# Attention output with the values and the state stationary: one head per column group, and the result transposed back

## The chip, the cores and the metric

The kernel runs on one NeuronCore of one Trainium2 chip. The metric is the time of one execution on the device, in microseconds (us). The kernel before was timed in three runs: 531.51, 533.49 and 534.09 us, median 533.49 us.

## The reference

Four batches, eight heads, 768 positions, 48 values per head. A gated linear attention comes first: a state of 48 x 48 per head decays by `alpha` and takes in the outer product of key and value at each position, and the output is the query times the state. Then the eight heads are laid side by side (384 columns), mixed by a Fourier transform over positions and columns, normalised, and sent through a feed-forward net with 384, 1536 and 384 columns.

```python
for t in range(S):
    state = alpha[:, :, t, :, None] * state + np.einsum('bhd,bhe->bhde', k[:, :, t], v[:, :, t])
    y[:, :, t] = np.einsum('bhd,bhde->bhe', q[:, :, t], state)
...
u = x + np.real(np.fft.fft(np.fft.fft(x, axis=1), axis=2))
un = (u - mean(u)) / np.sqrt(var(u) + 1e-06)
out = u + np.maximum(un @ w_ch1, 0.0) @ w_ch2
```

## The kernel before, in words

The attention is done for a pair of heads at a time, 16 pairs in all, four to a batch. Channels lie on the partitions: head 0 on partitions 0 to 47, head 1 on 64 to 111, so that a tile of a pair spans 112 partitions (`CW`); positions lie along the rows, in six blocks of 128. The stages of a pair (`attn_stages`) are:

- `s1` to `s3`: running products of `alpha` by two scans on VectorE (DVE), then keys divided by them (kept in the tile `al`) and queries multiplied by them (kept in a `w` tile, called `e["A"]`).
- `s4`: TensorE (PE) transposes the scaled keys, ScalarE (ACT) copies them to `kt`.
- `s5`: scores, keys times queries within a block of 128 positions. The two heads lie on different partitions, 48 or 64 rows each, and their matmuls stand next to each other in the program. ACT copies each head's scores from PSUM (into a tile `X`: `x` in the first batch, `w` later), GpSimd (POOL) masks them.
- `s6`: the state after each block. PE multiplies the transposed keys (stationary, 112 columns) by the values of both heads (moving, 96 columns): five matmuls. The products of one head's keys with the other's values are not wanted; two small ACT instructions make the decay factors `mh` with a zero for the wrong head, and a DVE product with them writes the tile `tt` of 112 partitions and 2 x 48 columns a block, with zeros for the wrong head. Four DVE instructions add up the blocks.
- `s7`: the output. For each block and head PE multiplies the scores (stationary, 128 columns) by the values (moving, 64 columns), and adds the queries (stationary, 112 rows and 128 columns) times the state `tt` (moving, 96 columns, both heads at once). The result has positions on the partitions, and ACT copies it to the tile `y`.

`combine` then prepares the transform on DVE; `mix_stages` does it on PE, `norm_stages` normalises, `ffn_stages` runs the feed-forward net. Its matmuls are the `f<-x,wt` and `f<-wt,h` of the profile: 128 x 128 stationary, 384 columns moving, 864 of each.

The order is made by a planner (`Plan`). Every operation is recorded with a duration from a formula (`duration`), a key and its dependencies; `emit` then places them one by one, on each engine the one with the smallest key among those that can start, and the engines run them in that order. The matmuls of a batch's feed-forward net have larger keys than the next batch's attention: they fill the time in which the attention waits. Up to `WARM` = 120 us of planned time the planner also puts small matmuls of zeros (128 rows, 32 columns stationary and moving, line 1130) where PE would be idle. Since one helper issues every operation, nearly all rows of the profile say line 471, and operations are told apart by their tiles. In a row, what stands after `<-` are the moving and then the stationary operand, and `128*112 128x96` is rows x columns of the stationary operand and rows x columns of the moving one. A matmul in float32 is two records.

A matmul uses a part of the PE array that follows from its operands: rows 48 or 64 (`s5`) give a shape of 64 rows, an output of 48 or 64 partitions a shape of 64 columns, one of 32 a shape of 32 columns; all else is the full array of 128 x 128.

Of the kernel before, what the change touches and what calls it, by code (L numbers as in the profile page):

```python
# [16 lines left out]
AF = mybir.ActivationFunctionType  # L17
ALU = mybir.AluOpType
AX = mybir.AxisListType

B, H, S, D = 4, 8, 768, 48
DM = H * D
DFF = 4 * DM
P = 128
NT = S // P
# [5 lines left out]
CW = 112  # L31
GRP = 64
# [141 lines left out]
class Plan:  # L174
# [119 lines left out]
    def duration(self, op, named, engine):  # L294
        n = op.free
        if "dma" in op.name:
            return 1.05 if engine == "POOL" else 0.05
        if engine == "PE":
            m = self.region(named["1"])[4]
            if op.name == "transpose":  # L300
                return max(m, self.region(named["2"])[4]) / 1200 + 0.002
            if str(named["1"].real(self.base(named["1"])).dtype).endswith("float32"):
                slow = 1.65 if self.stride(named["2"]) > 16 else 1.0
                p0, p1 = self.region(named["1"])[0:2]
                return max(m, slow * n) / (1100 if p1 - p0 <= GRP else 600) + 0.004
            return n / 2240 + 0.003
        if engine == "ACT":
            pointer = 0.094 if any(isinstance(named.get(k), View) for k in ("bias", "scale")) else 0.0
            slow = 1.8 if self.stride(named["out"]) > 16 and n > 64 else 1.0
            return (0.11 if self.psum(named.get("1")) else 0.14) + slow * n / 1200 + pointer + (0.25 if "accum_out" in named else 0.0)  # L310
        if op.name == "memset":
            return n / (960 if engine == "DVE" else 1100) + 0.01
        if engine == "DVE":
            if op.name == "bn_stats":
                return 0.47
            if op.name == "reciprocal":
                return 0.07 + n / 160
            if op.name == "tensor_tensor_scan":
                return 0.1 + n / 480
            if isinstance(named.get("scalar1"), View):  # L320
                return 0.09 + n / 1200
            whole = "bitcast" in [s[0] for s in named.get("out", View(None)).steps]
            pointer = 0.06 if isinstance(named.get("scalar"), View) else 0.0
            return 0.09 + pointer + n / (1920 if whole and op.name == "tensor_scalar" else 960)
        return 0.126 + n / 1094 if op.name == "affine_select" else 0.15 + n / 477
# [163 lines left out]
def gla_mix_ffn(ctx: ExitStack, tc: tile.TileContext, alpha, kq, v, w1, w2, consts, rowtab, out):  # L489
    nc = tc.nc  # L490
    plan = Plan({"PE": nc.tensor, "ACT": nc.scalar, "DVE": nc.vector, "POOL": nc.gpsimd, "SP": nc.sync})
    V, A, G, T, SY = (Engine(plan, e) for e in ("DVE", "ACT", "POOL", "PE", "SP"))
    FL = {k: Engine(plan, *[{"V": "DVE", "G": "POOL", "A": "ACT"}[c] for c in x]) for k, x in FX.items()}
# [31 lines left out]
    def psa():  # L525
        if state["start"]:
            state["i"] += 1
            return plan.tile(start_tags[state["i"] % 8])
        return plan.tile("a")
# [8 lines left out]
    def fixed(shape, name, dtype=F32):  # L538
        return plan.fixed(cp.tile(shape, dtype, name=name))
# [3 lines left out]
    ident = cst[:, ID_O : ID_O + P]  # L543
    wts = [None] * (NW // 2)
    loaded = {}
    tts = [fixed([P, NT - 1, 2, D], f"tt{i}") for i in range(2)]
    mhs = [fixed([P, NT - 1, 2], f"mh{i}") for i in range(2)]
    mts = [fixed([P, NT], f"mt{i}") for i in range(3)]
    d1 = fixed([P, S], "d1")
    back = fixed([P, S], "back")  # L550
# [3 lines left out]
    ceps = fixed([P, 1], "ceps")  # L554
    zero = fixed([P, 32], "zero")
    ones = fixed([P, 1], "ones")
    hm = fixed([P, 2], "hm")
    rows = fixed([P, 3], "rows", I32)
    bs = fixed([P, 1], "bs")
    fl = fixed([1, 1], "fl", I32)  # L560
# [42 lines left out]

    def setup():
        V.memset(zero, 0.0)
        for hd in range(2):
            V.memset(hm[GRP * hd : GRP * (hd + 1), hd : hd + 1], 1.0)
            V.memset(hm[GRP * (1 - hd) : GRP * (2 - hd), hd : hd + 1], 0.0)
        V.memset(d1, 0.0)
        V.memset(back, 0.0)  # L610
        V.memset(back[:, C - 1 :: 2 * C], 1.0)
        V.memset(cm63, -63.0)
        V.memset(ceps, 1e-6)
        for x in mts:
            V.memset(x, 0.0)
        V.memset(ones, 1.0)
        V.memset(bad, 0.0)
# [42 lines left out]
    def attn_stages(b, hp, i, mixed):  # L660
        tt, mt = tts[i], mts[hp % 3]
        pair = b * NP2 + hp
        e = {}
# [80 lines left out]
        def s6():  # L744
            pu = psa()
            for a in range(NT - 1):
                T.matmul(pu[0:CW, a * 2 * D : (a + 1) * 2 * D], e["kt"][:, a], loaded["vn", pair][:, 2 * a * D : 2 * (a + 1) * D], start=True, stop=True)
            mh = mhs[i]
            for hd in range(2):
                A.activation(mh[0:CW, :, hd], mt[0:CW, 0 : NT - 1], AF.Copy, scale=hm[0:CW, hd : hd + 1])  # L750
            V.tensor_tensor(
                out=tt[0:CW], in0=pu[0:CW, 0 : (NT - 1) * 2 * D].rearrange("p (a h e) -> p a h e", h=2, e=D),
                in1=mh[0:CW, :, :, None].broadcast_to([CW, NT - 1, 2, D]), op=ALU.mult,
            )
            for a in range(1, NT - 1):
                V.scalar_tensor_tensor(
                    out=tt[0:CW, a], in0=tt[0:CW, a - 1], scalar=mt[0:CW, a : a + 1], in1=tt[0:CW, a], op0=ALU.mult, op1=ALU.add,
                )

        def s7():  # L760
            X = e["X"]
            ytiles = mixed()[0]
            for h2 in range(2):
                py = psa()
                for c in range(3):
                    cc = 3 * h2 + c
                    cs = slice(cc * P, (cc + 1) * P)
                    o = c * 2 * GRP
                    for hd in range(2):
                        T.matmul(  # L770
                            py[:, o + hd * GRP : o + (hd + 1) * GRP], X[h2][:, hd, c], loaded["vn", pair][:, (2 * cc + hd) * D : (2 * cc + hd) * D + GRP],
                            start=hd == 0, stop=cc == 0 and hd == 1,
                        )
                    if cc:
                        yo = py[:, o : o + 2 * GRP].rearrange("p (h e) -> p h e", h=2)[:, :, 0:D]
                        T.matmul(yo, e["A"][0:CW, cs], tt[0:CW, cc - 1], start=False, stop=True)
                yo = py[:, 0 : 6 * GRP].rearrange("p (a h e) -> p a h e", a=3, h=2)[:, :, :, 0:D]
                FL["ev"].copy(ytiles[h2][:, :, hp * 2 * D : (hp + 1) * 2 * D].rearrange("p a (h e) -> p a h e", h=2), yo)

        return [s1, s2, s3, s4, s5, s6, s7, lambda: combine(*mixed(), hp * 2 * D, 2 * D, FL["comb"])]  # L780


# [273 lines left out]
    plan.key = -2000.0  # L1056
    load_consts(0)
    setup()
    load_first()
    for p in (1, 2, 3):  # L1060
# [30 lines left out]
    for i, f in enumerate(mixing()):  # L1091
        write([f], KF0 + 0.01 * i)
        n = MIX[i] if i < len(MIX) else 0
# [185 lines left out]
```

## Time and profile before

| | |
|---|---|
| median of 3 runs | 533.49 us |
| the profiled execution's own time | 536.18 us |
| its span, first to last instruction | 534.5 us |
| PE, share of the span busy | 96% |
| DVE, ACT, POOL | 65%, 37%, 14% |
| first and last matmul of the feed-forward net | 96.8 and 527.5 us |

The profile is one execution. A record on PE lasts longer than PE is taken up by it, because matmuls are pipelined: what one costs is read from the distance of starts, so from the start of a group in the timeline to the start of the next group, divided by its records. The records called `f` in the first batch are also attention, in other PSUM banks.

### The profile page before, as it was taken

What the parts mean: (1) busy time and instruction counts of PE and PEld (TensorE: products, weight loads), DVE (VectorE), ACT (ScalarE), POOL (GpSimd) and SP (SyncE); (2) the same over time, 40 slices, a digit from 0 to 9 for tenths busy, and PEclk for the clock granted to TensorE, in tenths of its full rate; (3) what the DMA queues carried; (4) which work ended last, traced back from release to release, by engine and by line L of the source; (5) the groups of instructions that cost most, each with busy time, mean ns of one, the idle gap of its engine ahead of it and who ended that gap; (6) DMA issues with size and microseconds to landing.
All of it is one profiled execution on the core that took longest, in us unless ns stands there. A gap on an engine that the chain in (4) does not pass through costs nothing.

```text
span 534.5 us, 10290 instructions
## 1 busy us (share of the span) xinstructions
PE 511.1 (96%) x4192; PEld 491.6 (92%) x4192; DVE 347.5 (65%) x835; ACT 195.7 (37%) x425; POOL 72.7 (14%) x99
## 2 busy tenths in 40 slices
PE   6899976999999999999999999999999999999994
PEld 5898975899999999899999999999999999999994
DVE  6767998688978999877579951676367613123112
ACT  1585566443456522643332232423321413111110
POOL 0115172021311300210220000111120000000000
PEclk9699989699999999999999999999999999999999
DMA  8991216020236410142342100120021001001001
GB/s 288 411 393 34 76 45 209 0 90 24 61 102 270 156 60 1 51 143 84 134 155 75 45 0 1 45 83 25 0 90 45 2 0 45 0 1 44 1 1 50
DMA packets 17127, 44.65 MB, mean 84 GB/s; under 512 B 1905, under 2 KB 7153, under 8 KB 17073
## 3 DMA queue, kind: packets, MB, share of 16 engines
q1 hardware_dynamic: 16016, 41.49, 21.7%
q0 software_dynamic: 768, 2.36, 1.5%
q8 instruction: 35, 0.57, 0.4%
q14 instruction: 20, 0.16, 0.1%
q10 hardware_dynamic: 288, 0.07, 0.1%
HBM read 36.83 MB, written 7.08 MB: 82 GB/s over the span
## 4 chain that ended last, share of the span: by engine, by line
PE 84%; POOL 4%; issue 3%; DMA 3%; ACT 3%; DVE 2%; SPq 0%; ACTq 0%; POOLq 0%
PE f L471 59%; PE a L471 22%; POOL y L471 2%; PE f L1130 2%; DMA al<-in_alpha_dram 2%; POOL x L471 1%; DMA wt<-in_w_dram 1%; ACT b L471 1%; DVE al L471 1%; ACT x L471 1%; POOL wt L471 1%; DVE y L471 1%; SPq L471 0%; ACT wt L471 0%; DVE z L471 0%
## 5 line engine op out<-in xcount | busy, mean ns | idle before, releaser
L471 PE MATMUL f<-x,wt 128*128 128x384 f32 x864 | 181.1, 346 | 0.1
L471 PE MATMUL f<-wt,h 128*128 128x384 f32 x864 | 180.1, 343 | 0.3 <-ACT h L210 0.3
L471 PEld LDWEIGHTS f<-x,wt 128*128 128x128 f32 x864 | 151.3, 190 | 1.7 <-ACT x L471 0.5
L471 PEld LDWEIGHTS f<-wt,h 128*128 128x128 f32 x864 | 150.4, 188 | 2.1 <-ACT h L210 0.4
L471 DVE SCALAR_TENSOR_TENSOR h<-f,h 128x384 fp32r<-128x384 f32 x96 | 53.3, 556 | 112.0 <-ACT h L210 111.3
L210 ACT ACTIVATE h<-f 128x384 fp32r<-128x384 f32 x96 | 47.0, 491 | 182.1 <-PE f L471 177.3
L471 POOL TENSOR_SCALAR_AFFINE_SELECT w<-w 128x384 f32<-128x384 f32 x48 | 27.7, 598 | 159.2 <-ACT w L471 159.2
L471 PE MATMUL a<-vn,w 128*128 128x64 f32 x288 | 41.3, 265 | 0.0
L1130 PEld LDWEIGHTS f<-zero 128*32 128x32 f32 x918 | 35.5, 122 | 5.7 <-issue 1.4
L1130 PE MATMUL f<-zero 128*32 128x32 f32 x918 | 38.7, 206 | 1.6 <-DVE zero L471 1.0
L471 PEld LDWEIGHTS a<-vn,w 128*128 128x128 f32 x288 | 39.6, 191 | 0.0
L471 ACT COPY w<-a 128x384 f32<-128x384 f32 (+4 forms) x60 | 26.7, 481 | 33.8 <-PE a L471 33.7
L471 DVE TENSOR_TENSOR sd<-y,y 128x288 f32<-128x288 f32 x32 | 13.6, 464 | 29.0 <-ACT y L471 28.9
L471 DVE TENSOR_TENSOR_SCAN w<-al,d 112x768 f32<-112x768 f32 (+1 forms) x17 | 28.5, 1675 | 4.0 <-POOL al L471 4.0
L471 POOL DMA_INDIRECT y<-scr,rows x12 | 23.2, 1936 | 44.0 <-DMA scr<-y 22.0
L471 DVE TENSOR_TENSOR_SCAN al<-al,back 112x768 f32<-112x768 f32 (+1 forms) x17 | 28.2, 1660 | 0.0
L471 PE MATMUL a<-tt,w 112*128 112x96 f32 x144 | 27.6, 279 | 0.3 <-DVE tt L471 0.3
L471 DVE TENSOR_TENSOR y<-y,a 128x191 f32<-128x191 f32 (+2 forms) x88 | 25.8, 344 | 0.9 <-PE a L471 0.7
L471 PE MATMUL a<-w,al 48*128 48x128 f32 (+1 forms) x306 | 25.9, 291 | 0.0
L471 PEld LDWEIGHTS a<-w,al 48*128 48x128 f32 (+1 forms) x306 | 20.0, 187 | 5.4 <-issue 2.0
L471 DVE TENSOR_TENSOR y<-y,f 128x384 f32<-128x384 f32 (+2 forms) x46 | 20.7, 481 | 5.7 <-PE f L471 5.7
L471 PEld LDWEIGHTS a<-tt,w 112*128 112x128 f32 x144 | 23.0, 190 | 1.1 <-DVE tt L471 0.4
(118 smaller groups left out, 576.9 us busy)
## 6 DMA issues: line engine op xcount, KB each, us to landing
kq<-in_kq_dram SPq DMA_DIRECT2D x13, 768.0 KB, 4.9
wt<-in_w_dram SPq DMA_DIRECT2D x8, 768.0 KB, 8.1
al<-in_alpha_dram SPq DMA_DIRECT2D x15, 384.0 KB, 5.0
out_dram<-y SPq DMA_DIRECT2D x24, 192.0 KB, 1.9
vn<-in_v_dram SPq DMA_DIRECT2D x14, 296.0 KB, 3.3
wt<-in_w_dram SPq DMA_DIRECT2D x8, 384.0 KB, 7.4
scr<-y SPq DMA_DIRECT2D x4, 576.0 KB, 3.7
wt<-in_kq_dram SPq DMA_DIRECT2D x2, 768.0 KB, 11.2
```

Of the source, the lines that this page charges most:

```text
L210: return lambda out, x: e.activation(out, x, AF.Relu)
L471: op.ins = op.fns[op.engine](*[real(a) for a in op.args], **{k: real(x) for k, x in op.kwargs.items()})
L1130: plan.idle = (lambda: nc.tensor.matmul(warm[2][0:32, 480:512], zero.real(), zero.real(), start=True, stop=True), 1.0, WARM, ("f2", 2))
```

## The change

The state update and the output are turned over, and each head has its own matmul.

- `s6`: for each block one matmul per head, the head's transposed keys stationary (64 columns for head 0, 48 for head 1), its own values moving (48 columns). The outputs lie on partitions 0 to 63 and 64 to 111. No product of different heads is made, so `mh`, `hm` and the ACT instructions that made them are gone, and `tt` has 48 columns a block where it had 96.
- `s7`: the values are stationary (64 or 48 columns), the scores move (128 columns); the state is stationary (48 rows and 48 columns at partitions 0 or 64), the queries move (128 columns), one matmul per head. The output has channels on the partitions, 112 x 384 for three blocks. ACT copies it into the scores' tile, three PE transposes turn it back, and the copy to `y` follows as before.
- The planner's formula takes 1100 instead of 600 for float32 matmuls whose stationary operand has at most 64 columns.

```diff
--- before.py
+++ after.py
@@ -302,7 +302,7 @@
                 slow = 1.65 if self.stride(named["2"]) > 16 else 1.0
                 p0, p1 = self.region(named["1"])[0:2]
-                return max(m, slow * n) / (1100 if p1 - p0 <= GRP else 600) + 0.004
+                return max(m, slow * n) / (1100 if p1 - p0 <= GRP or m <= GRP else 600) + 0.004
@@ -543,8 +543,7 @@
-    tts = [fixed([P, NT - 1, 2, D], f"tt{i}") for i in range(2)]
-    mhs = [fixed([P, NT - 1, 2], f"mh{i}") for i in range(2)]
+    tts = [fixed([P, NT - 1, D], f"tt{i}") for i in range(2)]
@@ -744,13 +739,14 @@
         def s6():
             pu = psa()
             for a in range(NT - 1):
-                T.matmul(pu[0:CW, a * 2 * D : (a + 1) * 2 * D], e["kt"][:, a], loaded["vn", pair][:, 2 * a * D : 2 * (a + 1) * D], start=True, stop=True)
-            mh = mhs[i]
-            for hd in range(2):
-                A.activation(mh[0:CW, :, hd], mt[0:CW, 0 : NT - 1], AF.Copy, scale=hm[0:CW, hd : hd + 1])
+                for hd, r in ((0, slice(0, GRP)), (1, slice(GRP, CW))):
+                    T.matmul(
+                        pu[r, a * D : (a + 1) * D], e["kt"][:, a, r], loaded["vn", pair][:, (2 * a + hd) * D : (2 * a + hd + 1) * D],
+                        start=True, stop=True,
+                    )
             V.tensor_tensor(
-                out=tt[0:CW], in0=pu[0:CW, 0 : (NT - 1) * 2 * D].rearrange("p (a h e) -> p a h e", h=2, e=D),
-                in1=mh[0:CW, :, :, None].broadcast_to([CW, NT - 1, 2, D]), op=ALU.mult,
+                out=tt[0:CW], in0=pu[0:CW, 0 : (NT - 1) * D].rearrange("p (a e) -> p a e", e=D),
+                in1=mt[0:CW, 0 : NT - 1, None].broadcast_to([CW, NT - 1, D]), op=ALU.mult,
             )
@@ -760,21 +756,27 @@
         def s7():
             X = e["X"]
             ytiles = mixed()[0]
+            heads = ((0, slice(0, GRP), slice(0, D)), (1, slice(GRP, CW), slice(GRP, CW)))
             for h2 in range(2):
                 py = psa()
                 for c in range(3):
                     cc = 3 * h2 + c
                     cs = slice(cc * P, (cc + 1) * P)
-                    o = c * 2 * GRP
-                    for hd in range(2):
+                    o = slice(c * P, (c + 1) * P)
+                    for hd, r, _ in heads:
+                        v0 = (2 * cc + hd) * D
                         T.matmul(
-                            py[:, o + hd * GRP : o + (hd + 1) * GRP], X[h2][:, hd, c], loaded["vn", pair][:, (2 * cc + hd) * D : (2 * cc + hd) * D + GRP],
-                            start=hd == 0, stop=cc == 0 and hd == 1,
+                            py[r, o], loaded["vn", pair][:, v0 : v0 + r.stop - r.start], X[h2][:, hd, c], start=True, stop=cc == 0,
                         )
                     if cc:
-                        yo = py[:, o : o + 2 * GRP].rearrange("p (h e) -> p h e", h=2)[:, :, 0:D]
-                        T.matmul(yo, e["A"][0:CW, cs], tt[0:CW, cc - 1], start=False, stop=True)
-                yo = py[:, 0 : 6 * GRP].rearrange("p (a h e) -> p a h e", a=3, h=2)[:, :, :, 0:D]
+                        for hd, _, r in heads:
+                            T.matmul(py[r, o], tt[r, cc - 1], e["A"][r, cs], start=False, stop=True)
+                yT = X[h2][0:CW, 0].rearrange("p c n -> p (c n)")
+                FL["ev"].copy(yT, py[0:CW, 0:DM])
+                pt = psa()
+                for c in range(3):
+                    T.transpose(pt[:, c * P : c * P + CW], yT[:, c * P : (c + 1) * P], ident[0:CW, 0:CW])
+                yo = pt[:, 0:DM].rearrange("p (a h e) -> p a h e", a=3, h=2)[:, :, :, 0:D]
                 FL["ev"].copy(ytiles[h2][:, :, hp * 2 * D : (hp + 1) * 2 * D].rearrange("p a (h e) -> p a h e", h=2), yo)
```

The planner lays out the new matmuls between those of the feed-forward net. Here is PE's order in the kernel before, in the last blocks of an output of the third batch: `tt` rows are queries times state, `vn` rows scores times values, `x,wt` and `wt,h` rows the feed-forward net, `al` rows other stages of the next pair (the scores, and in the `cst` rows transposes of its keys).

```order
L471 MATMUL f_1_398_2803<-x_338_2482,wt_0_131_1014 128x384 x3
L471 MATMUL a_389_2724<-tt_131,w_1_330_2423 128x2x48
L471 MATMUL a_389_2724<-vn_279_2053,w_4_378_2682 128x64 x2
L471 MATMUL a_389_2724<-tt_131,w_1_330_2423 128x2x48
L471 MATMUL a_400_2816<-cst,al_282_2066 128x112 x2
L471 MATMUL f_1_398_2803<-x_339_2486,wt_0_131_1014 128x384 x3
L471 MATMUL f_1_398_2803<-x_341_2491,wt_0_133_1035 128x384
L471 MATMUL a_391_2737<-tt_131,w_1_330_2423 128x2x48
L471 MATMUL a_391_2737<-vn_279_2053,w_3_385_2708 128x64 x2
```

All nine rows are in the full shape. The same place in the changed kernel, where `vn` is now the stationary operand and `64x128` and `48x128` are the outputs of the two heads:

```order
L471 MATMUL f_0_420_3036<-x_352_2625,wt_0_216_1700 128x384 x3
L471 MATMUL a_411_2956<-w_2_347_2600,tt_131 48x128 x2
L471 MATMUL a_411_2956<-w_1_398_2902,vn_296_2235 64x128
L471 MATMUL a_411_2956<-w_1_398_2902,vn_296_2235 48x128
L471 MATMUL f_0_420_3036<-x_353_2631,wt_0_234_1822 128x384 x3
L471 MATMUL a_411_2956<-w_2_347_2600,tt_131 48x128 x2
L471 MATMUL f_2_370_2732<-wt_0_234_1822,h_419_3024 128x384 x3
L471 MATMUL f_0_373_2740<-wt_0_234_1822,h_419_3024 128x384 x2
L471 MATMUL a_421_3040<-w_2_347_2600,tt_131 48x128 x2
L471 MATMUL a_421_3040<-w_4_403_2922,vn_296_2235 64x128
L471 MATMUL a_421_3040<-w_4_403_2922,vn_296_2235 48x128
L471 MATMUL a_421_3040<-w_2_347_2600,tt_131 48x128 x2
```

The heads' matmuls stand in twos, in shapes of 64 rows and 64 columns (`tt`) or 128 rows and 64 columns (`vn`), and between them stand matmuls of the full shape. Eight times in these twelve rows the next matmul has another shape than the one before it. Further on in the same output the plan also parts two heads, and puts the transposes of the first half between them:

```order
L471 MATMUL a_421_3040<-w_4_403_2922,vn_296_2235 48x128
L471 MATMUL a_421_3040<-w_2_347_2600,tt_131 48x128
L471 MATMUL a_423_3079<-cst,w_1_398_2902 128x112 x3
L471 MATMUL a_421_3040<-w_2_347_2600,tt_131 48x128
L471 MATMUL f_0_373_2740<-wt_0_234_1822,h_419_3024 128x384
```

The two `tt` rows are the two heads of one block; before, they were one matmul.

More of the change, by code (lines that the diff above doesn't have):

```diff
@@ L556, in gla_mix_ffn @@
     ones = fixed([P, 1], "ones")
-    hm = fixed([P, 2], "hm")
     rows = fixed([P, 3], "rows", I32)
@@ L605, in setup @@
         V.memset(zero, 0.0)
-        for hd in range(2):
-            V.memset(hm[GRP * hd : GRP * (hd + 1), hd : hd + 1], 1.0)
-            V.memset(hm[GRP * (1 - hd) : GRP * (2 - hd), hd : hd + 1], 0.0)
         V.memset(d1, 0.0)
@@ L767, in s7 @@
                     cs = slice(cc * P, (cc + 1) * P)
-                    o = c * 2 * GRP
-                    for hd in range(2):
+                    o = slice(c * P, (c + 1) * P)
+                    for hd, r, _ in heads:
+                        v0 = (2 * cc + hd) * D
                         T.matmul(
-                            py[:, o + hd * GRP : o + (hd + 1) * GRP], X[h2][:, hd, c], loaded["vn", pair][:, (2 * cc + hd) * D : (2 * cc + hd) * D + GRP],
-                            start=hd == 0, stop=cc == 0 and hd == 1,
+                            py[r, o], loaded["vn", pair][:, v0 : v0 + r.stop - r.start], X[h2][:, hd, c], start=True, stop=cc == 0,
                         )
                     if cc:
-                        yo = py[:, o : o + 2 * GRP].rearrange("p (h e) -> p h e", h=2)[:, :, 0:D]
-                        T.matmul(yo, e["A"][0:CW, cs], tt[0:CW, cc - 1], start=False, stop=True)
-                yo = py[:, 0 : 6 * GRP].rearrange("p (a h e) -> p a h e", a=3, h=2)[:, :, :, 0:D]
+                        for hd, _, r in heads:
[6 more added lines that the diff above has]
+                yo = pt[:, 0:DM].rearrange("p (a h e) -> p a h e", a=3, h=2)[:, :, :, 0:D]
                 FL["ev"].copy(ytiles[h2][:, :, hp * 2 * D : (hp + 1) * 2 * D].rearrange("p a (h e) -> p a h e", h=2), yo)
```

## The prediction

> **What bounds the kernel now.** First the page: busy time of each engine, PE over the span, and the chain that ended last.
>
> ```profile
> PE 511.1 (96%) x4192; PEld 491.6 (92%) x4192; DVE 347.5 (65%) x835; ACT 195.7 (37%) x425; POOL 72.7 (14%) x99
> PE   6899976999999999999999999999999999999994
> PE 84%; POOL 4%; issue 3%; DMA 3%; ACT 3%; DVE 2%; SPq 0%; ACTq 0%; POOLq 0%
> ```
>
> PE has gaps in the first seven slices and in the last, nowhere between, and 84% of the chain is PE. Which stretches are PE's alone is in the table of busy time by window (us, then busy us and instructions of PE, PEld, DVE, ACT, POOL):
>
> ```profile
> 110.00:222.00 112.00, 111.22 (x779) 106.78 (x778) 99.09 (x218) 50.92 (x111) 18.91 (x26) 1.00 0.28 96
> 222.00:336.00 114.00, 114.00 (x809) 110.58 (x808) 76.55 (x190) 38.35 (x93) 13.78 (x23) 1.00 0.22 77
> 336.00:450.00 114.00, 114.00 (x809) 110.61 (x808) 65.32 (x172) 33.07 (x78) 11.87 (x20) 1.00 0.10 32
> ```
>
> From 110 us on PE works without a hole at a granted clock of 1.00; no other engine fills a window. The feed-forward matmuls mark the stretch, in the view by tile of their weights (min/median/max ns, first and last start):
>
> ```profile
> L471 PE MATMUL f<-x,wt x864: 331/337/689, 96.8 to 524.3; 128*128 128x384 f32 x173
> L471 PE MATMUL f<-wt,h x864: 331/337/446, 104.5 to 527.5; 128*128 128x384 f32 x173
> ```
>
> From 96.8 to 527.5 us, 430.7 us, time is what PE's instructions cost; by the order of the program 12 of the 16 pairs are in it. What the change does to ACT and DVE there doesn't count while PE is full.
>
> **The prices on PE now.** Starts in the timeline give them. Two feed-forward groups, and the scores (64 and 48 rows, the two heads side by side) between full-array work:
>
> ```profile
> 339.26 1.13 PE L471 MATMUL f<-x,wt 128*128 128x384 f32 x5
> 340.32 0.94 PE L471 MATMUL a<-w,al 64*128 64x128 f32 x12
> 341.19 1.22 PE L471 MATMUL a<-vn,kt 128*112 128x96 f32 x10
> ...
> 358.99 1.74 PE L471 MATMUL f<-x,wt 128*128 128x384 f32 x9
> 360.56 1.73 PE L471 MATMUL f<-wt,h 128*128 128x384 f32 x9
> ```
>
> A feed-forward matmul costs (360.56 - 358.99) / 9 = 0.174 us. The state product and the output, in one pair:
>
> ```profile
> 369.95 1.13 PE L471 MATMUL a<-vn,kt 128*112 128x96 f32 x10
> 370.92 0.36 PE L471 MATMUL a<-vn,w 128*128 128x64 f32 x2
> ...
> 374.35 0.36 PE L471 MATMUL a<-tt,w 112*128 112x96 f32 x2
> 374.54 0.58 PE L471 MATMUL a<-vn,w 128*128 128x64 f32 x4
> 374.96 0.64 PE L471 MATMUL a<-tt,w 112*128 112x96 f32 x4
> 375.43 0.58 PE L471 MATMUL a<-vn,w 128*128 128x64 f32 x4
> ```
>
> The state's 10 records take 0.97 us, 0.097 each; the output's 10 records from 374.35 to 375.43 take 1.08, 0.108 each, with 64 columns moving as with 96. So the stationary side sets them, not the moving one. And small shapes, from the first batch:
>
> ```profile
> 23.55 0.43 PE L471 MATMUL a<-vn,x 128*128 128x64 f32 x2
> 23.91 0.56 PE L1130 MATMUL f<-zero 128*32 128x32 f32 x12
> 24.41 0.88 PE L471 MATMUL a<-vn,x 128*128 128x64 f32 x6
> ...
> 26.02 0.46 PE L471 MATMUL a<-cst,al 112*128 112x112 f32 x3
> 26.31 0.35 PE L471 MATMUL a<-vn,x 128*128 128x64 f32 x2
> ...
> 27.36 1.61 PE L471 MATMUL f<-w,al 64*128 64x128 f32 x24
> 28.90 0.25 PE L1130 MATMUL f<-zero 128*32 128x32 f32 x2
> ```
>
> Three transposes of a 112-row block take 0.29, 0.097 each. Scores: 24 records take 1.54 us (27.36 to 28.90), 12 take 0.87 (340.32 to 341.19); the 12 more cost 0.67, 0.11 for each step in which both heads run one record. So row groups do run at the same time: two records for the price of one.
>
> The same rows price **a change of shape**. 12 score records at 0.11 a step would be 0.66 but take 0.87: +0.21. The five feed-forward matmuls before them would be 0.87 but take 1.06: +0.19. The round trip of two changes is 0.40, so 0.20 a change when the neighbour is 384 columns wide. With columns it is less. The zeros (32 columns) run at 0.032:
>
> ```profile
> 60.25 0.46 PE L471 MATMUL f<-tt,w 112*128 112x96 f32 x2
> 60.64 7.09 PE L1130 MATMUL f<-zero 128*32 128x32 f32 x218
> 70.63 5.54 PE L471 MATMUL f<-cst,z 128*97 128x65 f32 x36 [2.90 <-DVE z L471]
> ```
>
> (7.09 less the last one's own 0.2, over 217.) At 23.91 twelve of them take 0.50 where 0.38 is their pace, +0.12, and the two output records before them take 0.36 where 0.22 is theirs, +0.14: 0.13 a change.
>
> **The change part by part**, for the 12 pairs in PE's stretch.
>
> *State.* Ten records of 0.097 become twenty, in pairs of column groups: ten steps. A step loads 64 columns. Loads of 128 columns cost 0.108 and of 32 columns 0.032, so I estimate 0.056 for 64, the moving 48 columns hiding behind it. 0.97 becomes 0.56: -0.41 a pair.
>
> *Output.* 34 records of 0.108, 3.67 us, become 44 in pairs, 22 steps. Now 128 columns move, as in the scores: 0.11 a step, 2.42. Six transposes come in at 0.097: 0.58. Together -0.67 a pair. Both: -1.08, times 12 is **-13.0**.
>
> *Partners lost.* Where the plan puts other work between the two heads, a matmul runs alone and its step carries one head. In the order of the changed program, from the first feed-forward matmul on, 42 score matmuls stand alone (2 before), 22 with the values stationary and 6 with the state: 68 more, two records each, half of each wasted: 68 x 0.11 = **+7.5**.
>
> *Changes of shape.* Counted along PE's order from the same matmul on: 72 before, 289 in the changed kernel, 217 more. By where they lead: 76 more back into the full shape (nearly all into 384-column matmuls), which I take at 0.19; 141 more into tile shapes (69 values, 59 state times queries, 12 state, 1 other), at 0.14, between the two prices since the columns to load are few. 14.4 + 19.7 = **+34.1**; with 0.13 for all it is 28, with 0.20 for all 43. No row shows a change between two tile shapes in this kernel; 65 of the 289 are such, and a free one would save 65 x 0.14 = 9. None of it can hide: PE has no idle time there.
>
> *ACT and DVE.* The groups that change:
>
> ```profile
> L471 ACT COPY w<-a 128x384 f32<-128x384 f32 x48 | 20.9, 482 | 19.4 <-PE a L471 19.3
> L471 ACT ACTIVATE mh<-mt,hm 112x5 f32<-112x5 f32 x32 | 8.2, 296 | 2.0 <-DVE tt L471 1.2 <-DVE mt L471 0.7
> L471 DVE TENSOR_TENSOR tt<-a,mh 112x480 f32<-112x480 f32 x15 | 9.8, 654 | 15.9 <-PE a L471 15.9
> L471 DVE SCALAR_TENSOR_TENSOR tt<-tt,mt 112x96 f32<-112x96 f32 x64 | 20.7, 325 | 0.6
> ```
>
> ACT loses two `mh` of 0.30 a pair and gains two copies like the first row, 0.48 each: +0.37. DVE's product halves in columns; against ops of the same kind that saves about 0.25, and the four sums at most half of 0.325 each: 0.25 to 0.9 a pair. Both lie under PE. The output comes later by a copy, three transposes and their waits, some 1.2 us. Behind it stand `combine` and the mixing, and the feed-forward matmuls of the batch before run meanwhile, so it costs nothing there. That cover is missing in the first batch: after the last `tt` at 60.25 PE has only zeros until the mixing at 70.63. There the 1.2 us lie on the path, ACT has 4 x 0.37 = 1.5 more, and the 49 further changes of shape before the feed-forward net (55 become 104) fall partly into waits. The lighter DVE work gives some back. I take **+2**, between 0 and 5.
>
> *Sum.* -13.0 + 7.5 + 34.1 + 2 = +30.6 on the profiled execution's 536.18: 566.8. That execution lies 2.7 above the median of 533.49, so for the median **564**.
>
> **The rivals.**
>
> *Column groups don't overlap.* Overlap is shown for rows only (scores); two column groups share all 128 rows, and the only column shape that the trace has, the zeros, always uses the same group. Then the state's twenty records run one by one, +0.56 x 12 = 6.7, and the 61 pairs with the values stationary pay their two steps again, 61 x 0.22 = 13.4; state times queries lies on different rows and stays paired. **584**. "TensorE: Matmul & The Clock Gate" of the Trainium skill, Part 3 (row and column tiling), reports 2.38 times the speed for three column groups; no run here shows it yet, and by it this rival falls.
>
> *Only the way into and out of the full array costs.* The 65 changes among tile shapes are free: **555**. For it: all priced changes have the full array on one side. Against: the 0.13 with the zeros looks like an emptying pipe, which wouldn't care where it goes.
>
> *Changes between column shapes cost almost nothing, and the kernel gets faster.* The place is PE's order around the output. Without the 34.1 the sum is -13.0 + 7.5 + 2 = -3.5, **530**. It decides from 3.5 / 217 = 0.016 us a change downwards, an eighth of the cheapest price above. For it: those prices stand at the edge of groups and hold a first load that a 64-column shape has less of. Against: 0.13 with a load of only 32 columns. "TensorEngine Tiling (Array Packing)" of the Trainium skill, Performance Considerations, recommends this very swap with column tiling, for up to twice the speed when the moving side has 64 columns or fewer. The same page, Tiling Modes, says that a change of mode drains the engine; the trace's 0.13 to 0.20 agree with that second rule.
>
> **How the numbers follow.** The forecast 0.58, no overlap 0.15, tile shapes free 0.13, changes free 0.09; 0.05 for changes at about half price with a first batch that gains, near 533 to 546. A measurement of this kernel can tell about 0.5% from no change. Faster comes from the free changes and a little of the last case, 0.10; within 0.5%, 0.04; slower, all else, 0.86. The range: below, 555 less the 6 us by which the price at 0.13 undercuts mine, and some of the last case, 546; above, 584 with 9 us for the price at 0.20, 592.
>
> **What would show it.** In the timeline of the changed kernel the records of the two heads with `vn` stationary start together, a step is 0.11 us, and the last record ahead of a group with another shape is followed by a gap of some 0.1 us and a slow second record. The stretch from first to last feed-forward matmul is some 459 us instead of 430.7, and PE stays full. Heads that start one after the other show the first rival; groups that follow at their own pace the third. If the first feed-forward matmul starts more than 5 us later than 96.8, the first batch was mis-sized. I am wrong if PE's stretch is not longer.

## The result, and the profile after

The changed kernel takes **564.81 us** (median of four runs, 564.02 to 565.72); the kernel before, on the same chip, 532.88 us (531.51 to 534.09). The ratio is 1.060, with a 95% interval of 1.057 to 1.063: the change makes the kernel 6% slower. Some executions run at a lower clock than the rest: the ratios leave them out, the medians and ranges of `e1_state` and `e6_full_shape` below hold one each, and the profile of `e1_state` is of that one (545.16 us), so that only its stretch after the first feed-forward matmul is used.

The lines of the page after that answer to those of before:

```profile
PE 541.4 (96%) x4682; PEld 472.0 (84%) x4682; DVE 339.3 (60%) x832; ACT 203.8 (36%) x425; POOL 75.8 (13%) x98
PE   7999976999999999999999999999999999999995
...
PE 89%; DVE 3%; ACT 3%; DMA 2%; issue 1%; SPq 0%; POOL 0%; ACTq 0%; POOLq 0%
```

PE is busy for 30 us more, and now 89% of the chain is PE. Its weight loads are busy for 20 us less. So PE's time went neither to more loading nor to waiting for another engine. The windows (us, then busy us and instructions of PE, PEld, DVE, ACT, POOL) and the feed-forward weights by tile, both of the changed kernel:

```profile
110.00:222.00 112.00, 112.00 (x833) 92.66 (x831) 82.97 (x190) 46.31 (x93) 17.50 (x23) 1.00 0.27 91
222.00:336.00 114.00, 113.83 (x861) 96.42 (x860) 74.64 (x194) 40.18 (x93) 16.90 (x23) 1.00 0.24 81
336.00:450.00 114.00, 114.00 (x871) 97.22 (x870) 61.87 (x156) 34.46 (x80) 12.50 (x21) 1.00 0.10 34
```

```profile
L471 PE MATMUL f<-x,wt x888: 272/337/689, 43.1 to 551.8; 128*128 128x384 f32 x173, 128*64 128x128 f32 x3, 128*48 128x128 f32 x2
L471 PE MATMUL f<-wt,h x864: 331/336/448, 106.5 to 554.9; 128*128 128x384 f32 x173
```

PE has next to no hole: 0.17 us in the second window. Weight loads filled 106.8 to 110.6 us of these windows before and fill 93 to 97 now, while PE stays at 112 to 114. So part of what the profile calls busy may be time in which PE makes no headway; whether the changes of shape are that time is what the experiments below test. The last feed-forward matmul starts at 554.9 us. The first row can't show where the stretch begins, since 24 records of the output now share its name; in the timeline the first one with 384 columns starts at 99.0 us. The stretch is 455.9 us where it was 430.7: **+25.3**. Its start is 2.2 us later, the tail behind it 0.3 longer; together 27.8, the difference of the two profiled executions (564.02 and 536.18).

Where the 25.3 us lie shows in the timeline of the changed kernel (start, duration, records of each group):

```profile
400.43 0.78 PE L471 MATMUL a<-vn,kt 128*64 128x48 f32 x20
401.14 0.44 PE L471 MATMUL f<-wt,h 128*128 128x384 f32 x1
401.51 0.65 PE L471 MATMUL a<-w,vn 128*64 128x128 f32 x8
402.09 1.14 PE L471 MATMUL f<-wt,h 128*128 128x384 f32 x5
403.07 1.73 PE L471 MATMUL f<-x,wt 128*128 128x384 f32 x9
...
405.99 0.42 PE L471 MATMUL a<-w,tt 48*48 48x128 f32 x4
406.34 0.43 PE L471 MATMUL a<-w,vn 128*64 128x128 f32 x4
406.70 0.64 PE L471 MATMUL a<-w,tt 48*48 48x128 f32 x8
407.28 0.43 PE L471 MATMUL a<-w,vn 128*64 128x128 f32 x4
```

- The state's twenty records take 0.71 us with a change of shape behind them. One after the other, at the prediction's 0.056 each, they would take 1.12; so the two column groups run at the same time. The single records of the trace agree: in the groups with `vn` or `tt` stationary the two heads' records start 0.006 to 0.007 us apart.
- Eight records with the values stationary take 0.58 us, four take 0.36. Four more records, two steps, cost 0.22, so a step is about 0.11, and in the four-record group 0.14 is left for the change of shape.
- One feed-forward record ahead of the values takes 0.37 (401.14 to 401.51) where its pace is 0.174: +0.20. Some of that is the way in from the state, some the way out to the values (the next section tells them apart).
- Going from `vn` to `tt` and back, with no full-array work between, costs 0.13 to 0.14 each time.

### The profile page after: what moved, and what is told of

Its sections match the earlier page's. It is cut to its first block, busy times and chain, and to the rows that moved or that the text cites. A ratio compares the mean times of both kernels' runs of the same rounds, so it can differ in the third digit from the quotient of the medians.

```text
span 562.3 us, 11297 instructions
## 1 busy us (share of the span) xinstructions
PE 541.4 (96%) x4682; PEld 472.0 (84%) x4682; DVE 339.3 (60%) x832; ACT 203.8 (36%) x425; POOL 75.8 (13%) x98
## 4 chain that ended last, share of the span: by engine, by line
PE 89%; DVE 3%; ACT 3%; DMA 2%; issue 1%; SPq 0%; POOL 0%; ACTq 0%; POOLq 0%
PE f L471 61%; PE a L471 26%; PE f L1132 3%; DMA al<-in_alpha_dram 1%; DVE f L471 1%; DVE y L471 1%; DVE wt L471 1%; DMA wt<-in_w_dram 1%; DVE z L471 0%; ACT b L471 0%; ACT L471 0%; SPq L471 0%; ACT wt L471 0%; POOL x L471 0%; ACT x L471 0%
## 5 line engine op out<-in xcount | busy, mean ns | idle before, releaser
L471 PE MATMUL f<-x,wt 128*128 128x384 f32 (+2 forms) x888 | 188.6, 346 | 0.2 <-DVE h L471 0.2
L471 PEld LDWEIGHTS f<-x,wt 128*128 128x128 f32 (+2 forms) x888 | 152.1, 187 | 8.2 <-issue 5.9
L471 ACT COPY w<-a 128x384 f32<-128x384 f32 (+3 forms) x84 | 38.2, 480 | 69.8 <-PE a L471 69.8
L471 POOL TENSOR_SCALAR_AFFINE_SELECT w<-w 128x384 f32<-128x384 f32 x48 | 33.8, 724 | 179.8 <-ACT w L471 179.8
L471 PE MATMUL a<-w,vn 128*64 128x128 f32 (+1 forms) x288 | 32.8, 292 | 0.0
L471 PE MATMUL a<-w,al 48*128 48x128 f32 (+1 forms) x312 | 30.7, 290 | 0.0
L471 PEld LDWEIGHTS a<-w,al 48*128 48x128 f32 (+1 forms) x312 | 24.5, 187 | 6.9 <-issue 3.5
L471 PE MATMUL a<-w,tt 48*48 48x128 f32 x280 | 29.9, 287 | 0.0
L471 PEld LDWEIGHTS a<-w,vn 128*64 128x64 f32 (+1 forms) x288 | 15.9, 128 | 14.1 <-issue 13.2
L471 PEld LDWEIGHTS a<-w,tt 48*48 48x48 f32 x280 | 12.4, 118 | 13.7 <-issue 9.5
```

The source lines that it names most:

```text
L471: op.ins = op.fns[op.engine](*[real(a) for a in op.args], **{k: real(x) for k, x in op.kwargs.items()})
```

## The experiments

In the tables below "changes" and "alone" are counted along PE's order from the first feed-forward matmul on: matmuls with another shape than the one ahead of them, and matmuls whose other head doesn't stand next to them. "Stretch" is from the first to the last matmul with 384 columns. In kernels with a further helper the lines are called 494 and 253 where the others say 471.

### What a change of shape costs by itself

The kernel before, with 96 small matmuls put between those of the last feed-forward net (in PE's order some come to stand side by side). Their result is used nowhere. In the first kernel they have 32 columns stationary, as the zeros have:

```diff
+ if state.get("extra") and n in (2, 4, 6, 8):
+     T.matmul(plan.tile("a")[0:32, 0:32], zero, x[dc][xi][:, 0:32].bitcast(F32), start=True, stop=True)
```

> The kernel before with 96 added matmuls in the last batch's feed-forward net, four in each of 24 first-layer tiles: 32 columns stationary (zeros), 32 moving, outcome unused. Each takes 2 x 0.032 us at its pace. Theory: the shape changes on the way in and out cost 0.11 + 0.20 more; by PE's order there are 157 changes more (some of the added stand side by side): +31 us, 564. Rival (a change of shape is free): 96 x 0.064 = +6, 539.

In the second they have 128 columns stationary, four times as much to load, and stay in the full shape:

```diff
-     T.matmul(plan.tile("a")[0:32, 0:32], zero, x[dc][xi][:, 0:32].bitcast(F32), start=True, stop=True)
+     T.matmul(plan.tile("a")[0:P, 0:32], ident, x[dc][xi][:, 0:32].bitcast(F32), start=True, stop=True)
```

> The same 96 added matmuls with 128 columns stationary (the identity) and 32 moving: the full shape, so no change of shape, but four times the columns to load, 2 x 0.11 us each. Both theories: 96 x 0.22 = +21, 554. What tells them apart is the comparison: by the theory the smaller matmuls cost 10 us more than these, by the rival 15 us less.

Measured: 571.03 us with the small shape (563.66 to 572.02; ratio 1.069, 1.059 to 1.079), 553.65 with the full one (552.87 to 562.59; 1.040, 1.035 to 1.046). The timelines, small shape first:

```profile
508.90 0.44 PE L471 MATMUL f<-x,wt 128*128 128x384 f32 x1
509.27 0.25 PE L471 MATMUL a<-x,zero 128*32 128x32 f32 x2
509.45 0.44 PE L471 MATMUL f<-x,wt 128*128 128x384 f32 x1
509.82 0.25 PE L471 MATMUL a<-x,zero 128*32 128x32 f32 x2
```

```profile
491.94 0.51 PE L471 MATMUL f<-x,wt 128*128 128x384 f32 x2
492.29 0.30 PE L471 MATMUL a<-x,cst 128*128 128x32 f32 x2
492.43 0.59 PE L471 MATMUL f<-x,wt 128*128 128x384 f32 x2
```

A feed-forward record between two small shapes takes 0.37, with two changes at its ends; in the full shape two records take 0.35, their plain pace. The smaller matmul costs more. In the stretch, the small shape adds 460.4 - 430.7 = 29.7 us. Its 192 records at the pace of the zeros, 0.032, are 6.1; the small matmuls stand in 79 groups, so the other 23.6 are 158 changes: **0.149 us a change**, as a mean of ways in and ways out. The full shape adds 449.9 - 430.7 = 19.3, 0.10 a record, and its 553.65 is the 554 expected. The mean hides a difference. Between two changes a single feed-forward record takes 0.20 more than its pace (0.37 for 0.174), two of the small records 0.12 more (0.18 for 0.064), and four records of the changed kernel's tiles 0.13 to 0.14 more (0.35 to 0.36 for 0.22). The starts of single records in the traces tell more: ahead of a change the last record holds PE 0.09 us longer, whatever follows (a feed-forward record 0.268 for 0.175, a record with `vn` stationary 0.202 for 0.109); behind it the second record comes later by 0.11 among 384-column records (0.281 for 0.175) and by 0.02 to 0.05 in shapes of 32 and 64 columns.

The 571.03 lie above the 564 expected because the first batch of the profiled execution was late, not because of a dearer change: one of the three executions took 563.66, at a mean clock of 0.979, the other two 571.03 and 572.02, at 0.964 and 0.962. That part of the program is the same as before, yet its first feed-forward matmul starts at 101.5 us where before has 96.8, and the clock between 20 and 100 us is 0.82 where before has 0.91 (the third number from the end of the row; before, then small shape):

```profile
20.00:100.00 80.00, 71.22 (x1086) 65.81 (x1086) 67.58 (x169) 50.17 (x96) 26.81 (x23) 0.91 0.45 161
```

```profile
20.00:100.00 80.00, 70.95 (x971) 66.00 (x969) 61.10 (x153) 45.99 (x83) 25.65 (x19) 0.82 0.44 158
```

### The two halves of the change alone

Only the state turned: `s6` as in the change, the output and `mh` as before. Both halves have the planner's new formula.

```diff
+ T.matmul(pu[r, a * D : (a + 1) * D], e["kt"][:, a, r], loaded["vn", pair][:, (2 * a + hd) * D : (2 * a + hd + 1) * D], start=True, stop=True)
```

> The kernel before with the state update alone turned over (one matmul per head in column groups, its outcome spread over both heads' columns by the old masked product), the output as before. Theory (each change of the matmul's shape on PE costs 0.13 to 0.20 us, column groups overlap): the state stands mostly right behind the scores, so along PE's order from the first feed-forward matmul there are 85 changes of shape instead of 72; 13 more at 0.15 cost 2, the halved state saves 0.41 a pair on 12 pairs, 4.9: 2 to 3 us faster than before, 530 to 531. Rival (the turned matmuls and what hangs on them are slow in themselves, shapes or not): slower than before, by about a quarter of the change's 32 us, 540.

Only the output turned, the state as before:

```diff
+ py[r, o], loaded["vn", pair][:, v0 : v0 + r.stop - r.start], X[h2][:, hd, c], start=True, stop=cc == 0,
...
+ T.matmul(py[r, o], tt[r, cc - 1, hd], e["A"][r, cs], start=False, stop=True)
```

> The kernel before with the output alone turned over (values and state stationary, transposed back), the state update as before. Theory: 277 changes of shape from the first feed-forward matmul on, 58 matmuls of a pair of heads that stand apart: +33 in PE's stretch, 566 to 568, as slow as the whole change or a little slower. Rival (the turned matmuls are slow in themselves): the rest of the change's 32 us, 557.

Measured: the state alone 536.47 (534.92 to 545.16; 1.008, 1.005 to 1.010), the output alone 580.49 (579.86 to 581.79; 1.091, 1.087 to 1.096). Both miss. The state alone lies some 6 above what was expected, on the other side of the kernel before, and its rival's 540 missed as well. The output alone misses by 13. It is slower than the whole change, though the number of changes of shape is less (277 to 289). Its timeline shows what no term of the sum had: holes on PE where it waits for the first transposes of the next batch.

```profile
231.31 0.45 PE L471 MATMUL a<-cst,al 112*128 112x112 f32 x3
232.54 0.38 PE L471 MATMUL a<-cst,al 112*128 112x112 f32 x2 [0.78 <-DVE r L471]
233.84 0.33 PE L471 MATMUL a<-cst,f 128*128 128x128 f32 x1 [0.92 <-ACT f L471]
234.44 0.33 PE L471 MATMUL a<-cst,f 128*128 128x128 f32 x1 [0.27 <-ACT f L471]
235.36 1.76 PE L471 MATMUL a<-cst,f 128*128 128x128 f32 x7 [0.59 <-ACT kt L471]
```

```profile
225.00:255.00 30.00, 27.29 (x124) 23.02 (x123) 20.41 (x57) 11.18 (x28) 2.43 (x6) 0.72 0.17 60
```

In this window PE is idle for 2.7 us, and the granted clock is 0.72: 0.28 x 30 = 8.4 us more are lost to the clock, which the trace shows at 0.50 for 17.1 us from 235.1 us on, behind the first holes. Together 11.1 of the 13. The expectation also speaks of 58 parted matmuls where the table below has 78, 2 us at 0.105 each; whether its +33 held them is not on record. The state alone has a smaller loss of this kind: a hole of 1.71 us ahead of a group that waits for ACT, 2.8 us idle and a clock of 0.86 in ten us, 4.2 in all. This is the profile of the execution of 545.16 us; that the other ten, of 534.92 to 538.44, lose as much there is not shown.

```profile
227.18 0.62 PE L471 MATMUL f<-x,wt 128*128 128x384 f32 x2 [1.71 <-ACT x L471]
```

```profile
221.00:231.00 10.00, 7.21 (x40) 6.09 (x39) 9.46 (x24) 7.05 (x16) 0.12 (x1) 0.86 0.17 61
```

The changed kernel and the kernel before have no such fall of the clock there. The plan decides whether the feed-forward net of one batch still has work when the next batch's first transposes wait for DVE and ACT; why the plan runs short here in these two, and in `e12_output_wide` and `e7_half` below, was not tried, nor why the clock stayed down for 17.1 us in the one and 3.4 in the other.

### Is a change between two tile shapes dear as well?

The output alone again, with the state stationary on all 112 rows (it still holds zeros for the wrong head). Then `vn` and `tt` have the same shape, 128 rows and 64 columns.

```diff
- T.matmul(py[r, o], tt[r, cc - 1, hd], e["A"][r, cs], start=False, stop=True)
+ T.matmul(py[r, o], tt[0:CW, cc - 1, hd], e["A"][0:CW, cs], start=False, stop=True)
```

> The output alone turned, as in the run of that name, but the state as stationary operand takes all 112 rows and the queries of both heads move (the state still holds zeros for the wrong head): values and state then have the same shape of 128 rows and 64 columns, and going from one to the other is no change. By the order of the program 222 changes instead of 277; no further matmul and no other size. Theory (a change between two tile shapes costs as much as any, 0.14 to 0.15): 55 x 0.145 = 8 us less than the output alone turned, 572 to 573. Rival (only the way into and out of the full array costs): those 55 were free, so no gain, 579 to 581.

Measured: 572.09 us (571.70 to 573.40; 1.072, 1.070 to 1.075), 8.4 less than the output alone, as the theory says (6.2 less in the stretch of the profiles, which here holds 1.1 more of holes and lost clock). The timeline:

```profile
402.70 0.43 PE L471 MATMUL a<-w,tt 112*48 112x128 f32 x4
402.96 0.39 PE L471 MATMUL a<-w,vn 128*64 128x128 f32 x4
403.18 0.39 PE L471 MATMUL a<-w,tt 112*48 112x128 f32 x4
403.40 0.38 PE L471 MATMUL a<-w,vn 128*64 128x128 f32 x2
```

From `vn` to `tt` and on to `vn`, four records take 0.22, two steps of 0.11 and nothing else. In the changed kernel the same four take 0.35 to 0.36. The 0.13 to 0.14 between them is a change from one tile shape to another, and the rival by which only the full array costs has fallen. "TensorEngine Tiling (Array Packing)" of the Trainium skill, Tiling Modes, says that a change of mode, not of tile alone, drains the engine; these two timelines agree.

### Fewer changes, same matmuls

Three kernels with all the matmuls of the change, in another order. The first has the planner's old formula:

```diff
- return max(m, slow * n) / (1100 if p1 - p0 <= GRP or m <= GRP else 600) + 0.004
+ return max(m, slow * n) / (1100 if p1 - p0 <= GRP else 600) + 0.004
```

> The change with the planner's duration formula as it was before, nothing else undone; only the order changes. Theory: 259 changes of shape instead of 289, and a little fewer parted heads: adding the prices along PE's order gives 6 us less than the whole change, about 558. Rival (order doesn't matter, the instructions are the same): 565, no change against the whole change.

In the other two a new helper `plan.group` records a list of matmuls as one operation, so that the planner can't put anything between them. The scores of three blocks, the state product of a pair, and the output are such groups, in the output all `vn` ahead of all `tt`. In `e7_half` the output of half a pair is a group (code shortened, remarks added):

```diff
+ plan.group(items)              # scores of three blocks, both heads
+ plan.group([...])              # state product, both heads
+ for part in ((0,), (1,)):
+     ...
+     plan.group(first + second) # output: first all vn, then all tt
```

> As the run with a pair's output in one block, but one block for each half of the positions: the shapes change twice as often around the output, 151 changes instead of 118, with the same matmuls. Theory: by the prices +4.7 against that run, 531 to 533. Rival (what counts is only that the heads of a block stay together): the same 527.

In `e4_pair` the output of a whole pair is one group (from the second batch on):

```diff
- for part in ((0,), (1,)):
+ for part in (((0, 1),) if b else ((0,), (1,))):
```

> The change with the same matmuls, copies and transposes, but the planner places a pair's output as one block (first all matmuls with the values stationary, then all with the state stationary, both halves of the positions; each half for itself in the first batch), and a half's scores and a pair's state update as one block each. Theory: 118 changes of shape from the first feed-forward matmul on instead of 289, no parted heads: the prices along PE's order give 7 us less than the kernel before in PE's stretch; with up to 2 lost in the first batch 526 to 530, faster than both. Rival (the turned matmuls, the transposes and the longer way to y are slow in themselves): 555 or more, since all of them are still there.

Measured: 556.12 (555.31 to 560.39; 1.047, 1.042 to 1.053) with the old formula, 533.71 (531.51 to 535.66; 1.004, 1.001 to 1.007) with groups per half, 527.41 (524.76 to 531.18; 0.991, 0.988 to 0.994) with groups per pair; all within 2 us of what was expected, and all three rivals missed. The last computes just what the change computes, with 118 changes of shape in place of 289, and is faster than the kernel before, by 0.9%. So the loss comes from the order, not from the turned matmuls.

### Is it the turned matmuls or the groups that gain?

The kernel before with the same groups and nothing turned:

```diff
+ items.append(((yo, e["A"][0:CW, cs], tt[0:CW, cc - 1]), dict(start=False, stop=True)))
+ ...
+ plan.group(items)
```

> The kernel before with nothing turned over, but the same blocks in the planner: a pair's output in one block (each half in the first batch), a half's scores and the state update as one block each. Theory: 62 changes instead of 72 and nothing else saved, -1.3 by the prices: 531 to 534. Rival (the run with the turned matmuls in blocks was faster because of the blocks): 527.

Measured: 529.72 (526.80 to 531.44; 0.994, 0.991 to 0.997), between theory and rival: the groups alone gain 0.6%, some 3 us (0.8% when timed again below). Both kernels were then timed again, with a third that cuts the turned output's group in two:

> The change with its matmuls in blocks (a pair's scores, state product and output each placed as one), run again beside the same blocks of the kernel before. Theory: with the changes of shape down to 118 in the stretch (62 in the blocks of the kernel before), the turned matmuls save their own -13.0 us less 56 changes at about 0.16 (9) and less the partners' loss, which is 0 now: by these prices 4 to 5.6 us less in the stretch than the other. Of that the earlier looks showed some 2. I expect 526 to 528, 2 to 4 below the kernel with the same blocks and nothing turned. Rival: turning gains nothing even in blocks, the whole gain is the blocks': within 1 us of the other kernel.

> The kernel before with the same blocks and nothing turned. Theory: 529 to 530, so 2 to 4 above the change in blocks. Rival: within 1 us of it.

```diff
- plan.group(first + second)
+ plan.group(first)
+ plan.group(second)
```

> The change in blocks, with the output's block cut in two: all matmuls with the values stationary, then, as a block of its own, all with the state stationary, so that the plan may put other work between them. By the order of the program there are again 118 changes of shape from the first feed-forward matmul on and no matmul without its partner. Theory (only changes and lone matmuls count): the same as in one block, 526 to 528. Rival: smaller blocks leave fewer holes (2 us at 158.6 us of the one-block kernel), so 523 to 525.

Measured: turned 527.58 (525.24 to 531.23; 0.989, 0.985 to 0.992), not turned 528.72 (526.79 to 530.30; 0.992, 0.989 to 0.994), turned with the group cut 523.70 (521.19 to 525.23; **0.983, 0.980 to 0.985**). The first two can't be told apart: 1.1 us lie between them where 2 to 4 were expected, and their intervals overlap. Their stretches are equal too (427.5 and 427.6 us), though the turned kernel's holds some 3.5 us of holes and lost clock that the other's has not. The third is the fastest of all kernels here, 1.7% below before, and its interval lies clear of that of the kernel with nothing turned, and all but clear of that of the one-group kernel (0.985 is the edge of both); there the rival was right, not the theory by which only changes and partners count. The timeline of the one-group kernel shows what its rival named:

```profile
155.30 2.26 PE L494 MATMUL f<-wt,h 128*128 128x384 f32 x11
159.27 2.25 PE L494 MATMUL f<-wt,h 128*128 128x384 f32 x7 [1.72 <-DVE h L494]
```

```profile
158.00:164.00 6.00, 4.73 (x18) 4.73 (x19) 5.20 (x12) 1.30 (x4) 0.46 (x1) 0.72 0.52 212
```

PE waits 1.72 us for DVE, and then the trace shows the clock at 0.50 for 3.4 us: 0.72 in the window. The profile of `e4_pair`, the same kernel, shows the same. In the kernel with the cut group this window is full at clock 1.00, and no later one in its stretch has a lower clock:

```profile
158.00:164.00 6.00, 6.00 (x66) 5.32 (x67) 4.60 (x15) 3.39 (x7) 2.09 (x4) 1.00 0.00 0
```

The stretches of the two profiles differ by 5.4 us, some 3.5 of it this hole, its clock and a smaller wait. But these are profiles of the longest execution of the one kernel and the shortest of the other (531.23 and 521.19 us). The shortest of the one-group kernel took 525.24 at a mean clock of 0.989, where the profiled one has 0.973; how often the clock falls there, and so how much of the 3.9 us between the medians is the hole, stays open.

Here the pair's groups show what the turned matmuls can do; a group's time up to the start of the next one holds most of its two changes of shape:

```profile
328.34 0.78 PE L253 MATMUL a<-vn,kt 128*64 128x48 f32 x20
329.05 0.44 PE L494 MATMUL f<-x,wt 128*128 128x384 f32 x1
...
332.57 1.52 PE L253 MATMUL a<-w,vn 128*64 128x128 f32 x24
334.03 0.80 PE L494 MATMUL f<-x,wt 128*128 128x384 f32 x3
...
338.45 1.30 PE L253 MATMUL a<-w,tt 48*48 48x128 f32 x20
339.68 1.14 PE L494 MATMUL f<-wt,h 128*128 128x384 f32 x5
```

0.71 + 1.46 + 1.23 = 3.40 us a pair, 3.98 with the six transposes at 0.097, where the kernel before paid 0.97 + 3.67 = 4.64. Whether the kernel before would gain as much from a cut of its own output groups was not tried, so how much of the 5.0 us between 523.70 and 528.72 is the turning stays open.

### All of it in one sum

The stretch of each kernel, by the prediction's terms with the measured sizes: 429.9 us (430.7 less the 0.8 that PE idles in before, 215 to 225 us), the turned matmuls at the prediction's -13.0 (state -4.9, output -8.0), 0.105 for each further lone matmul, 0.15 for each further change of shape, and PE's holes with the clock lost behind them, from the windows (in `e1_state` those of the execution of 545.16 us). The kernel before has 72 changes and 2 lone matmuls.

| kernel | changes | alone | holes, us | sum | stretch, us |
|---|---|---|---|---|---|
| changed | 289 | 70 | 0 | 456.6 | 455.9 |
| `e3_formula` | 259 | 58 | 0 | 450.8 | 450.4 |
| `e7_half` | 151 | 0 | 4.4 | 432.9 | 432.2 |
| `e4_pair` | 118 | 0 | 4.4 | 428.0 | 427.9 |
| `e11_values_then_state` | 118 | 0 | 0.4 | 424.0 | 422.2 |
| `e1_state` | 85 | 6 | 4.2 | 431.6 | 433.3 |
| `e2_output` | 277 | 78 | 11.1 | 471.7 | 472.3 |
| `e12_output_wide` | 222 | 78 | 12.2 | 464.6 | 466.1 |
| `e10_blocks_again` | 62 | 0 | 0 | 428.2 | 427.6 |

None of the nine is more than 1.8 us off, over a range of 50. The price of a change comes from the small matmuls, not from these kernels; it is the mean price, the same for every change.

## Why the prediction was right

The mechanism was right, and so was the time (564 predicted, 564.81 measured), but that it was right to within 1 us is luck: two errors cancel. The terms one by one:

- **The two halves of the matmuls, -13.0.** Right. The heads run together, and the rival without overlap, 584, has fallen. "TensorE: Matmul & The Clock Gate" of the Trainium skill, Part 3 (row and column tiling), reports a gain from column groups; the state's twenty records in 0.71 us agree.
- **Partners lost, +7.5.** Right in kind; a step measures 0.105 to 0.11, so 7.1 to 7.5. With no lone matmul (`e7_half`, `e4_pair`) the term is gone, and the sum still holds.
- **Changes of shape, +34.1.** Right in kind and nearly in size. At the mean price of 0.149 the 217 are 32.3. The choice of 0.19 for the way back into 384-column matmuls and 0.14 for the way into tiles stands up: with the 0.09 ahead of a change counted to the shape that follows, single records give 0.20 and 0.11 to 0.14.
- **The stretch.** Some 459 us predicted, 455.9 measured: 3.3 too much. 0.8 of it is idle time of PE in the kernel before that is gone in the changed one; the prediction says that PE works without a hole from 110 us on, but its own first window row has 111.22 us of 112. Up to 1.8 come from the price of a change, the rest from a step at 0.105 for 0.11 and within what the sum can tell.
- **The first batch, +2.** The two traces show 2.2. This is not as good as it looks: the first feed-forward matmul of kernels that are the same up to there starts anywhere from 94.5 (full small matmuls) to 101.5 us (small shape), as the clock goes. The medians differ by 31.9, where the traces differ by 27.8. So 564 against 564.81 sets two errors against each other: a stretch priced 3.3 too long, and a first batch that in the medians costs more than 2, some 6 if all the rest lies there. Which of the two figures it is stays open, since medians have no trace.
- **The rivals.** That only changes into and out of the full array cost (555) fell with the wide state. The prediction says that no row of the kernel before shows a change between two tile shapes; its rows at 27.36 and 28.90 do, scores and then zeros, and there the trace has 0.20 from the last score record to the first zero where the pace is 0.105. So this rival was weaker from the start than its 0.13. The upper end of the range is off by one: 584 and 9 make 593, not 592. That changes cost nothing (530) fell in the timeline; but it named the right lever. "TensorEngine Tiling (Array Packing)" of the Trainium skill, Performance Considerations, recommends the swap with column tiling: once the changes are down to 118 and no hole is left, the swapped kernel does take 523.70.
- What the prediction had nowhere is that a hole of PE can cost a multiple of itself by the clock. It did not matter for the changed kernel, whose stretch has no hole to speak of, but it made up most of the miss of `e2_output`.

## What to carry to other kernels

Before splitting a matmul into column or row tiles, count along PE's order how often the shape will change, and set each change (0.15 us here on average) against what a pair saves (0.11 a step): a split of two blocks that stand alone between full-array matmuls loses. Do the same matmuls in one block, heads next to each other, so that a whole group pays for one way in and one way out. When blocks are made larger, look for the holes that they leave: shorter blocks, cut where a shape changes anyway, were worth 3.9 us here by the medians, with intervals that just touch.

## What the runs showed of the hardware that was not expected

- A change of shape costs 0.149 us on average, between two tile shapes as well. 0.09 of it lies ahead of the change, whatever the shapes; what lies behind it goes with what follows, 0.11 for 384-column records in the full shape, 0.10 for the scores, 0.02 to 0.05 for 32 to 64 stationary columns. A matmul of a quarter of the columns costs more than a full one if it stands singly or in twos in another shape: 96 of them added 29.7 us to the stretch, against 19.3 for the full ones.
- Behind single waits of PE of 1.71 and 1.72 us (the state alone, one group per pair) the granted clock fell to 0.50 for 3.4 us, and took about as much again from the kernel; behind the 0.64 us wait before, it didn't. "TensorE: Matmul & The Clock Gate" of the Trainium skill, Part 1, speaks of an idle window of some 3.4 us. Here less than that in one piece was enough, with other short waits near it in the state alone, and in the one-group kernel without any other between 158 and 164 us.
- Two column groups share all 128 rows, and yet two heads' records load and run side by side: with the values stationary they start 0.007 us apart, and the pair takes one step of 0.11 us.
